# Group 0: when GpSimd's third masking of V starts, and who copies the transposed weights

## The chip, the cores and the metric

One core of a Trainium2 chip runs the whole program. Its engines are TensorE (PE: matmuls and transposes), VectorE (DVE), ScalarE (ACT), GpSimd (POOL) and SyncE (SP, which here only issues DMAs). Each engine works through its own queue in order and waits on semaphores for the others. The metric is the device time of one execution in microseconds (us); the number used is the median over several executions.

## The reference

Attention over keys and values that are pooled eight to one, followed by a two-layer network with a tanh GELU:

```python
k_p = k.reshape(B, H, Sp, pool, D).mean(axis=3)          # B=8, H=8, S=576, D=64, pool=8, Sp=72
v_p = v.reshape(B, H, Sp, pool, D).mean(axis=3)
scores = scale * np.matmul(q, k_p.transpose(0, 1, 3, 2))
attn = np.exp(scores - np.max(scores, axis=-1, keepdims=True))
attn = attn / (np.sum(attn, axis=-1, keepdims=True) + 1e-09)
attn_out = np.matmul(attn, v_p)
x = attn_out.transpose(0, 2, 1, 3).reshape(B * S, H * D)  # 4608 x 512
h = x @ w_in                                              # 512 x 2048
g = 0.5 * h * (1.0 + np.tanh(c * (h + 0.044715 * h * h * h)))
out = g @ w_out                                           # 2048 x 512
```

## The kernel before

The 4608 tokens are cut into nine groups of 512: group g < 8 holds the first 512 tokens of batch g, and a ninth group holds the 64 tokens left over from each batch. A group goes through attention and then through the two layers. Attention of the next group is threaded between the matmuls of the running group by hand: `at(hooks, s, f, ...)` places a call before matmul step s, and the whole program is issued in exactly the order written (`manual_schedule`). For group 0 there is nothing to thread it between, so its attention (lines 689 to 738) is the start-up of the kernel, and TensorE reaches the first layer only when it is through.

In group 0 the 512 queries are worked in four blocks j of 128, two blocks at a time (a half). For each block:

- `cast_q` turns queries into bf16, `q_transpose_pe(g, j, eng, tag)` transposes four 128x128 pieces on TensorE into PSUM (`tp`), and `eng` copies them to `qT`.
- `scores(g, j)` makes four matmuls into `sc`, and `exps(g, j)` lets ScalarE write `e`, the exponentials of eight heads with 72 keys each (128x576).
- `norm_two(g, j, 5)` (lines 284 to 294): VectorE sums `e` (`den`, L264), takes the reciprocal (`r`, L289) and scales the first five heads into `eb` (L291, 128x360); ScalarE scales the other three heads (L294, three instructions).
- `e_transpose_pe(g, j, eng, tag)` (lines 299 to 303) transposes the normalised weights `eb` in five pieces on TensorE, and `eng` copies them to `eT`. A copy is L94 on VectorE or GpSimd and L92 on ScalarE, whatever is copied.
- `values_half(0, 0, x, ...)` multiplies `eT` of blocks 0 and 1 with `vbd` into `xo`; x = 0 uses slots 0 to 3 of `vbd`, x = 1 slots 4 to 7. `xo` is copied to `xT`, from which the first layer (L394, `hidden_half`) starts.

`vbd` is the pooled V, laid out block-diagonally by heads. `spread_v` (lines 167 to 185) makes it with five multiplications by a 0/1 mask (each times 1/8 for the mean): part 0 is two of them, part 1 is one (the third masking), part 2 the last two. For group 0 they run on GpSimd.

The order of GpSimd's queue around the change is: two `w_in` loads, part 0, part 1, the cast of the queries of blocks 2 and 3, part 2, two more `w_in` loads (quarters 2 and 3 of the first layer's weights). The first layer uses quarter 2 in its third stretch of 16 matmuls, and quarter 3 in its fifth. TensorE's queue is: transposes of weights 0, of queries 2 and 3, of weights 1, `scores(0, 2)`, `values_half` for x = 0 and 1, `scores(0, 3)`, first layer. PSUM tiles with tag "mm" rotate through four buffers, so the order of the calls also sets who waits for whose buffer.

SyncE's loads of group 1 wait on line 748, a tiny DMA that reads quarter 1 of `w_in` and writes the tile `gate`. The tile `gate` is elsewhere the target of one-element copies on GpSimd which exist only to make GpSimd wait for what they read (`cast_gated`, `spread_gated`, `gate_queries`).

Of the kernel before, what the change touches and what calls it, by code (L numbers as in the profile page):

```python
# [19 lines left out]
def kernel(  # L20
# [21 lines left out]
    nc = tc.nc  # L42
# [8 lines left out]
    W = H * Sp  # L51
# [18 lines left out]
    eb = consts.tile([128, 4, 5 * 128], BF16, name="eb")  # L70
# [10 lines left out]
    gate = consts.tile([128, 1], BF16, name="gate")  # L81
# [8 lines left out]
    def copy(eng, out, in_):  # L90
        if eng is nc.scalar:
            eng.copy(out=out, in_=in_)  # L92
        else:
            eng.tensor_copy(out=out, in_=in_)  # L94
# [33 lines left out]
    def cast_q(g, j0, j1, eng):  # L128
        if "qb" not in st[g]:
            st[g]["qb"] = work.tile([128, 4, H, D], BF16, name="q_b", bufs=1)  # L130
        copy(eng, st[g]["qb"][:, j0:j1], st[g]["q"][:, :, j0:j1].rearrange("p h j d -> p j h d"))
# [22 lines left out]
    def pool_pe(b, c0, c1, copies, eng):  # L154

        n = c1 - c0
        ps = psum.tile([128, 2, D], F32, name="vp", tag="mm", bufs=4)
        for i in range(8):
            nc.tensor.matmul(out=ps[:, 0:n], lhsT=identf, rhs=st[b]["kv"][:, c0:c1, i, :], start=(i == 0), stop=(i == 7))  # L159
        kvb = st[b]["kvb"]  # L160
        copy(eng, kvb[:, c0:c1, 0:copies, :], ps[:, 0:n].unsqueeze(2).to_broadcast([128, n, copies, D]))
# [5 lines left out]
    def spread_v(b, eng, parts=(0, 1, 2)):  # L167
        kvb = st[b]["kvb"]

        def mult(n0, n1, c0, t0, p0):  # L170
            m = (n1 - n0) // 2
            eng.tensor_tensor(out=vbd[p0:128, b, n0:n1, :].rearrange("p (c r) (hh d) -> p c (r hh) d", c=max(m, 1), d=D),  # L172
                              in0=kvb[p0:128, 4 + c0:4 + c0 + max(m, 1), 0, :].unsqueeze(2).to_broadcast(
                                  [128 - p0, max(m, 1), 4 if m else 2, D]),
                              in1=vmask[p0:128, c0:c0 + max(m, 1), t0:t0 + (4 if m else 2)].unsqueeze(3).to_broadcast(
                                  [128 - p0, max(m, 1), 4 if m else 2, D]), op=ALU.mult)

        if 0 in parts:
            mult(0, 1, 0, 2, 64)
            mult(1, 3, 1, 0, 0)  # L180
        if 1 in parts:
            mult(3, 5, 2, 0, 0)
        if 2 in parts:
            mult(5, 7, 3, 0, 0)
            mult(7, 8, 4, 0, 0)
# [37 lines left out]
    def q_transpose_pe(g, j, eng, tag):  # L223
        tp = psum.tile([128, HP, 128], BF16, name="tp", tag=tag, bufs=BUFS[tag])
        for pr in range(HP):
            nc.tensor.transpose(out=tp[:, pr, :],
                                in_=st[g]["qb"][:, j, 2 * pr:2 * pr + 2, :].rearrange("p h d -> p (h d)"),
                                identity=identb)
        copy(eng, st[g]["qT"][:, j], tp)
# [5 lines left out]
    def scores(g, j):  # L235
        sc = psum.tile([128, 2, MAIN], F32, name="sc", tag="sc", bufs=2)
        qT = st[g]["qT"]
        for pr in range(HP):
            if g == 0:
                o = sc[:, pr // 2, 2 * Sp * (pr % 2):2 * Sp * (pr % 2) + 2 * Sp]  # L240
                nc.tensor.matmul(out=o, lhsT=qT[:, j, pr, :], rhs=kbd[:, g, pr].rearrange("d hh s -> d (hh s)"),
                                 start=True, stop=True)
                continue

            for hh in range(2):
                for p0 in (0, 64):
                    h0 = 64 * hh
                    nc.tensor.matmul(out=sc[p0:p0 + 64, hh, Sp * pr:Sp * pr + Sp],  # L248
                                     lhsT=qT[h0:h0 + 64, j, pr, p0:p0 + 64],
                                     rhs=kbd[h0:h0 + 64, g if g < B else 2 * j + p0 // 64, pr, hh],  # L250
                                     start=True, stop=True)
        st[g][("sc", j)] = sc
# [31 lines left out]
    def norm_two(g, j, h0):  # L284

        e = st[g][("e", j)]
        sums(g, j)
        r = work.tile([128, H], F32, name="r")
        nc.vector.reciprocal(out=r, in_=st[g].pop(("den", j)))  # L289
        o = eb[:, j, 128 * 5 - W:].rearrange("p (h s) -> p h s", s=Sp)  # L290
        nc.vector.tensor_tensor(out=o[:, 0:h0], in0=e[:, 0:h0], in1=r[:, 0:h0].unsqueeze(2).to_broadcast([128, h0, Sp]),  # L291
                                op=ALU.mult)
        for h in range(h0, H):
            nc.scalar.activation(out=o[:, h], in_=e[:, h], func=ACT.Copy, scale=r[:, h:h + 1])  # L294
# [4 lines left out]
    def e_transpose_pe(g, j, eng, tag):  # L299
        tp = psum.tile([128, 5, 128], BF16, name="tp", tag=tag, bufs=BUFS[tag])  # L300
        for c in range(5):
            nc.tensor.transpose(out=tp[:, c, :], in_=eb[:, j, 128 * c:128 * c + 128], identity=identb)
        copy(eng, st[g]["eT"][:, j], tp)
# [412 lines left out]
    norm_two(0, 0, 5)  # L716
    spread_v(0, nc.gpsimd, (0,))
    pool_pe(0, 7, 9, 1, nc.scalar)
    spread_v(0, nc.gpsimd, (1,))
    cast_q(0, 2, 4, nc.gpsimd)  # L720
    spread_v(0, nc.gpsimd, (2,))
    load_w_in(2)
    load_w_in(3)
    norm_two(0, 1, 5)
    e_transpose_pe(0, 0, nc.scalar, "mm")
    q_transpose_pe(0, 2, nc.vector, "mm")
    q_transpose_pe(0, 3, nc.scalar, "mm")
    e_transpose_pe(0, 1, nc.vector, "mm")
    scores(0, 2)
    exps(0, 2)  # L730
    for x in range(2):
# [214 lines left out]
```

## Time and profile before

| What | Value |
|---|---|
| median of 4 runs | 279.49 us (278.79 to 280.01) |
| the profiled execution's own time | 278.79 us |
| its span, first to last instruction | 276.9 us |
| TensorE busy (PE), share of the span | 269.3 us, 97% |
| VectorE busy | 223.6 us, 81% |
| ScalarE busy | 175.9 us, 64% |
| GpSimd busy | 80.3 us, 29% |
| TensorE clock granted, mean | 1.000 |

The profile is of one execution. Its page has the engines' busy time, the span cut into 40 slices, the chain of work that ended last, and the costliest groups of instructions. A group's line reads: program line, engine, operation, tile written <- tile read, shape, count. The trace behind it gives single instructions by time. These lines of the page show how the first of 40 slices (6.9 us each) differ from the rest, in tenths of busy time for each engine:

```profile
PE   7989999999999999999999999999999999999995
DVE  5886869999966799989998999899989558955832
ACT  1586576488546764696479646963696469656820
POOL 4740272006420542314231426663223300300000
PEclk9999999999999999999999999999999999999999
```

TensorE is below nine tenths only in the first slices, 0 to about 21 us, and at the very end. The change lies between 12 and 17 us.

### The profile page before, as it was taken

How to read it: one execution, taken by the hardware profiler on the slowest of the kernel's cores; microseconds unless marked ns; L12 is line 12 of the kernel's file. 1: busy time of each engine (PE TensorE's matmuls, PEld its weight loads, DVE VectorE, ACT ScalarE, POOL GpSimd, SP SyncE). 2: the span in 40 equal slices, each digit the busy share in tenths (PEclk: the TensorE clock that was granted, in tenths of full speed). 3: DMA queues.
4: the chain of work that ended last, by engine and by line, in shares of the span. 5: the costliest groups of instructions: out<-in, count | busy, mean ns of one | idle time of the engine just before them, and what ended most of it. 6: DMA issues, size and time to landing. Idle time of an engine off the chain costs nothing.

```text
span 276.9 us, 6571 instructions
## 1 busy us (share of the span) xinstructions
PE 269.3 (97%) x2686; PEld 192.2 (69%) x2686; DVE 223.6 (81%) x365; ACT 175.9 (64%) x265; POOL 80.3 (29%) x121
## 2 busy tenths in 40 slices
PE   7989999999999999999999999999999999999995
PEld 3668844446854587668866876687668966886684
DVE  5886869999966799989998999899989558955832
ACT  1586576488546764696479646963696469656820
POOL 4740272006420542314231426663223300300000
PEclk9999999999999999999999999999999999999999
DMA  7999999999999896899479969995852460243013
GB/s 228 311 197 284 367 386 228 285 369 227 252 200 244 260 279 140 177 315 228 133 169 286 264 128 216 220 246 153 175 154 47 125 151 2 50 101 100 1 41 114
DMA packets 67857, 54.37 MB, mean 196 GB/s; under 512 B 41459, under 2 KB 53747, under 8 KB 67827
## 3 DMA queue, kind: packets, MB, share of 16 engines
q1 hardware_dynamic: 65186, 50.67, 71.3%
q0 software_dynamic: 2496, 3.15, 6.4%
q8 instruction: 21, 0.34, 0.5%
q10 hardware_dynamic: 144, 0.13, 0.1%
q14 instruction: 10, 0.07, 0.1%
HBM read 36.70 MB, written 9.44 MB: 167 GB/s over the span
## 4 chain that ended last, share of the span: by engine, by line
PE 86%; DVE 7%; DMA 4%; ACT 2%; issue 1%; SPq 0%; DVEq 0%; ACTq 0%
PE mm L586 28%; PE mm L383 22%; PE c L474 13%; PE mm L399 5%; PE mm L394 5%; PE xo L344 3%; PE x L586 3%; PE sc L248 2%; DMA eT<-eb 2%; DMA kv<-in_k_dram 2%; DVE den L264 1%; PE mm L531 1%; PE vp L159 1%; DVE eb L279 1%; ACT gT L490 1%; PE xo L355 1%
## 5 line engine op out<-in xcount | busy, mean ns | idle before, releaser
L383 PE MATMUL mm<-xT,w_in_b 128*128 128x512 bf16 x304 | 69.9, 379 | 0.0
L586 PEld LDWEIGHTS <-gT 128*128 128x128 bf16 x512 | 48.3, 98 | 9.1 <-issue 1.4
L385 ACT ACTIVATE gT<-mm 128x512 bf16<-128x512 f32 x76 | 43.6, 599 | 14.9 <-PE mm L383 14.6
L383 PEld LDWEIGHTS <-w_in_b 128*128 128x128 bf16 x304 | 29.8, 98 | 30.7
L586 PEld LDWEIGHTS <-stage 128*128 128x128 bf16 x384 | 37.5, 98 | 4.6 <-DVE stage L438 0.2
L279 POOL TENSOR_TENSOR eb<-e,r 128x576 bf16<-128x576 f32 x14 | 16.1, 1151 | 58.1 <-DVE r L273 46.1
L92 ACT CAST xT<-xo 128x512 bf16<-128x512 f32 (+1 forms) x24 | 13.2, 610 | 29.0 <-PE xo L344 24.6
L586 PE MATMUL mm<-tw,gT 128*128 128x256 bf16 x240 | 30.0, 273 | 0.0
L586 PE MATMUL mm<-w_out_b,gT 128*128 128x256 bf16 x240 | 29.9, 273 | 0.0
L264 DVE TENSOR_REDUCE den<-e 128x8 f32<-128x576 f32 x36 | 26.2, 727 | 2.9 <-ACT e L257 2.9
L257 ACT ACTIVATE e<-sc 128x576 f32<-128x576 f32 x36 | 22.5, 650 | 8.8 <-POOL eb L279 7.0
L149 DVE TENSOR_TENSOR kv<-kv 128x1024 f32<-128x1024 f32 (+3 forms) x19 | 23.7, 1247 | 4.2 <-DMA kv<-in_k_dram 3.1
L586 PE MATMUL mm<-tw,stage 128*128 128x256 bf16 x224 | 26.7, 273 | 0.0
L92 ACT COPY osb<-mm 128x512 f32<-128x512 f32 x30 | 17.8, 592 | 13.0 <-PE mm L586 12.4
L172 POOL TENSOR_TENSOR vbd<-kvb,vmask 128x256 bf16<-128x256 bf16 (+2 forms) x38 | 22.6, 616 | 7.3 <-DVE kvb L152 6.3
L474 PEld LDWEIGHTS <-ws 128*128 128x128 bf16 x192 | 18.8, 98 | 6.1
L94 POOL CAST q_b<-q_sb 128x1024 bf16<-128x1024 f32 (+1 forms) x15 | 15.6, 1058 | 20.3 <-DMA q_sb<-in_q_dram 20.3
L279 DVE TENSOR_TENSOR eb<-e,r 128x576 bf16<-128x576 f32 x18 | 18.0, 1002 | 0.6
L474 PE MATMUL c<-tt,ws 128*128 128x256 bf16 x144 | 17.7, 273 | 0.0
L434 DVE TENSOR_TENSOR stage<-gT 128x512 bf16<-128x512 bf16 (+1 forms) x25 | 13.2, 528 | 4.1 <-ACT gT L385 2.4
L435 DVE TENSOR_TENSOR gT<-gT 128x512 bf16<-128x512 bf16 (+1 forms) x25 | 13.0, 519 | 3.5 <-ACT gT L385 1.4
L94 POOL COPY kbd<-kTd 64x288 bf16<-64x288 bf16 x12 | 6.1, 504 | 33.2 <-DMA kTd<-kvb 32.9
(107 smaller groups left out, 424.2 us busy)
## 6 DMA issues: line engine op xcount, KB each, us to landing
kv<-in_k_dram SPq DMA_DIRECT2D x7, 1024.0 KB, 8.2
q_sb<-in_q_dram SPq DMA_DIRECT2D x7, 1024.0 KB, 10.1
kv<-in_v_dram SPq DMA_DIRECT2D x6, 1024.0 KB, 9.5
out_dram<-osb SPq DMA_DIRECT2D x12, 512.0 KB, 3.0
out_dram<-osb SPq DMA_DIRECT2D x11, 256.0 KB, 3.3
kv<-in_v_dram SPq DMA_DIRECT2D x4, 512.0 KB, 10.2
w_in_b<-in_moe_w_in_dram POOLq DMA_DIRECT2D x4, 512.0 KB, 6.8
w_out_s<-in_moe_w_out_dram SPq DMA_DIRECT2D x2, 1024.0 KB, 13.2
```

The source lines that it names most:

```text
L92: eng.copy(out=out, in_=in_)
L94: eng.tensor_copy(out=out, in_=in_)
L149: add(out=t[:, :, 0:4, :], in0=t[:, :, 0:4, :], in1=t[:, :, 4:8, :], op=ALU.add)
L172: eng.tensor_tensor(out=vbd[p0:128, b, n0:n1, :].rearrange("p (c r) (hh d) -> p c (r hh) d", c=max(m, 1), d=D), in0=kvb[p0:128, 4 + c0:4 + ...
L257: nc.scalar.activation(out=e.rearrange("p (x h) s -> p x (h s)", x=2), in_=sc[:, :, 0:4 * Sp], func=ACT.Exp, scale=1.0 / 64.0)
L264: nc.vector.reduce_sum(out=den, in_=e, axis=AX.X)
L279: eng.tensor_tensor(out=o.rearrange("p (pr hh s) -> p hh pr s", hh=2, s=Sp), in0=e.rearrange("p (hh pr) s -> p hh pr s", hh=2), in1=r.rear ...
L383: nc.tensor.matmul(out=hp, lhsT=w_in_b[:, ko, fo * 128:(fo + 1) * 128], rhs=st[g]["xT"][:, ko, :], start=(i == 0), stop=(i == KO - 1))
L385: nc.scalar.activation(out=gT[:, fo, :], in_=hp, func=ACT.Gelu_apprx_tanh)
L394: nc.tensor.matmul(out=hp[:, f, :], lhsT=w_in_b[:, ko, (fo + f) * 128:(fo + f + 1) * 128], rhs=st[g]["xT"][:, ko, c0:c0 + 256], start=(ko ...
L474: nc.tensor.matmul(out=acc[:, m, :], lhsT=lhs(i, m), rhs=rhs(i), start=bool(fresh and i == 0 and m % 2 == 0), stop=(i == 1), skip_group_ch ...
L586: nc.tensor.matmul(out=xs[p] if acc is xs else acc[:, p, :], lhsT=lt, rhs=rt, start=bool(fresh and m == 0 and (p == 0 or (last and acc is ...
```

## The change

A one-element copy on GpSimd is put ahead of the third masking. It reads the first element (head 0, key 0) of block 0's normalised weights in `eb`, which VectorE's first normalisation writes. So GpSimd's third masking, and everything behind it in GpSimd's queue, starts after that normalisation. Further, the transposes of the weights of blocks 0 and 1 are called one after the other, ahead of those of queries 2 and 3; the copy of block 0's goes from ScalarE to VectorE, and that of block 1's from VectorE to ScalarE.

```diff
     norm_two(0, 0, 5)
     spread_v(0, nc.gpsimd, (0,))
     pool_pe(0, 7, 9, 1, nc.scalar)
+    nc.gpsimd.tensor_copy(out=gate, in_=eb[:, 0, 128 * 5 - W:128 * 5 - W + 1])
     spread_v(0, nc.gpsimd, (1,))
     cast_q(0, 2, 4, nc.gpsimd)
     spread_v(0, nc.gpsimd, (2,))
     load_w_in(2)
     load_w_in(3)
     norm_two(0, 1, 5)
-    e_transpose_pe(0, 0, nc.scalar, "mm")
+    e_transpose_pe(0, 0, nc.vector, "mm")
+    e_transpose_pe(0, 1, nc.scalar, "mm")
     q_transpose_pe(0, 2, nc.vector, "mm")
     q_transpose_pe(0, 3, nc.scalar, "mm")
-    e_transpose_pe(0, 1, nc.vector, "mm")
     scores(0, 2)
     exps(0, 2)
```

## The prediction, made before the changed kernel ran

> **What bounds the kernel now.** I read the chain of waits first. From 23 us to the end it is nearly all TensorE (86% of the span by the page), with no wait on a load, so whatever moves the first `xo` of group 0 moves the end by the same amount. Start in us, length in us, engine, tile and line:
>
> ```profile
> 12.37 0.98 DVE eb L291
> 13.35 0.67 DVE den L264
> 14.04 0.21 DVE r L289
> 14.30 0.05 issue
> 14.34 0.84 ACT eb L294 x3
> 15.19 0.58 ACT eT L92
> 15.76 0.49 ACT qT L92
> 16.26 0.04 issue
> 16.30 0.62 PE xo L317 x4
> ```
>
> The reader is to see that VectorE's two normalisations (L291) with a sum and a reciprocal between them set the pace, and that `xo` starts at 16.30. It also needs the second block's transposed weights, whose VectorE copy ends at 16.24. Second, the timeline of VectorE and GpSimd over the same stretch, and two later places with the same operations:
>
> ```profile
> 12.37 0.98 DVE L291 TENSOR_TENSOR eb<-e,r 128x360 bf16<-128x360 f32 x1
> 13.27 0.74 DVE L264 TENSOR_REDUCE den<-e 128x8 f32<-128x576 f32 x1
> 14.28 0.92 DVE L291 TENSOR_TENSOR eb<-e,r 128x360 bf16<-128x360 f32 x1
> 18.57 0.76 DVE L276 TENSOR_TENSOR eb<-e,r 128x576 bf16<-128x576 f32 x1
> 38.68 1.36 DVE L279 TENSOR_TENSOR eb<-e,r 128x576 bf16<-128x576 f32 x1
> ```
>
> ```profile
> 12.35 0.61 POOL L172 TENSOR_TENSOR vbd<-kvb,vmask 128x256 bf16<-128x256 bf16 x1
> 13.18 1.07 POOL L94 CAST q_b<-q_sb 128x1024 bf16<-128x1024 f32 x1 [0.21 <-DMA q_sb<-in_q_dram]
> 14.21 0.61 POOL L172 TENSOR_TENSOR vbd<-kvb,vmask 128x256 bf16<-128x256 bf16 x1
> 15.41 1.55 POOL L654 DMA_DIRECT2D w_in_b<-in_moe_w_in_dram  x2
> 38.39 1.04 POOL L94 CAST w_out_b<-w_out_s 128x1024 bf16<-128x1024 f32 x1
> ```
>
> A normalisation of 576 takes 0.76 with GpSimd idle (18.57), but one of only 360 takes 0.98 and 0.92 beside a masking. Scaling by VectorE's f32 additions (128x512 0.69, 128x256 0.42: 1.05 ns an element and 0.15 fixed) 360 elements are worth 0.53. So the two lose 0.45 and 0.39. The loss is a wait, not a slower rate: 12.37 + 0.45 = 12.82, which is 0.14 before the masking's recorded end (12.96); 14.28 + 0.39 = 14.67, 0.15 before 14.82. At 38.68 the partner is a cast: 1.36 - 0.76 = 0.60 of wait ends at 39.28, again 0.15 before its end (39.43). The sum (L264) keeps its 0.74 beside a cast. So I read: whichever of GpSimd's operation and VectorE's two-input operation starts first finishes, the other waits; 0.02 us of lead (12.35 against 12.37) was enough.
>
> **The change part by part.**
>
> *The hold.* The third masking no longer starts at 12.35. The first normalisation then runs clean: 12.37 to 12.90, a gain of 0.45. Sum, reciprocal and second normalisation follow with the old spacing (its start was 0.93 after the first's end): 13.83.
>
> *The new copy into `gate`* is one instruction on GpSimd. Existing one-element copies begin 0.07 after the VectorE result they wait for (75.04 to 75.11), last 0.18 (64x1 bf16) or 0.25 (128x1 f32) undisturbed, 0.59 when VectorE is in a two-input operation, and the next GpSimd operation follows 0.27 after the start of the 0.18 one. In the new order VectorE is in the sum then, so I take 0.27 and keep 0.59. Behind it in GpSimd's queue wait the third masking, the cast of the queries 2 and 3 (whose data land at 13.18, so it loses its old start), two maskings and two `w_in` loads with all that needs them. Third masking 12.97 + 0.27 = 13.24, cast 0.57 later (the step of 11.78 to 12.35): **13.81**, end 14.86.
>
> *The second normalisation meets the cast.* It wants to start at 13.83, the cast at 13.81. That is closer than I can call exactly, so both ends:
> (a) cast first: VectorE waits to 14.86 - 0.15 = 14.71 and ends at 15.24, against 15.20 before. The gain of 0.45 is gone at once.
> (b) VectorE first: it ends at 14.36; ScalarE's three pieces end at 14.73 (reciprocal ends 0.45 earlier, and so do they, bar the 0.01 by which ScalarE comes free). The cast is pushed to 14.36 - 0.13 + 1.05 = 15.28 (0.13 from the masking at 46.65, which sat behind the addition of 46.42).
> A gate of 0.59 gives third masking 13.56, its hold to 14.02, normalisation to 14.55, cast end 15.47: like (b), 0.19 later.
>
> *The new order of transposes and copies.* No instruction is added; weights of block 1 now stand before the queries in TensorE's queue. With T the end of the second normalisation: weights' transposes at T + 0.06 (15.20 to 15.26 before), issue 0.27 for five, then query 2's; first transpose to the start of its copy 0.43 (9.09 to 9.52), VectorE's copy 0.41, +0.06 to `scores(0, 2)` (15.54 to 15.60), four matmuls 0.24, then `xo`. So `xo` = T + 0.06 + 0.27 + 0.43 + 0.41 + 0.06 + 0.24 = T + 1.47, where it was T + 1.10. Before, the query copy (15.13 to 15.54) lay in the shadow of the second normalisation; now it is behind it: **0.37 given away** whatever T is. ScalarE's copy of block 1 (0.67) starts at T + 0.06 + 0.49 and ends at T + 1.22, hidden behind the query path; VectorE's copy of block 0 (0.49) ends near T + 0.45, hidden too. Were the query path shorter, `xo` could not start before T + 1.28.
> (a): 15.24 + 1.47 = 16.71, **+0.41**. (b): queries' transposes wait for the cast, 15.28 + 0.05 (14.25 to 14.30 before) + 0.43 + 0.41 + 0.06 + 0.24 = 16.47, +0.17; with the long gate +0.36.
> I take (a), because the gate's nearest row puts the cast ahead and a lead of 0.02 decided before.
>
> *The last two maskings* start behind the normalisation in (a) and end near 16.2; the `xo` that needs them comes at 17.1, so they cost nothing with 0.9 of cover.
>
> *The two `w_in` loads* go from 15.41 to about 16.15 (0.75 later). Nothing moved passes SP's queue: its wait is for the second `w_in` quarter, issued at 10.37 ahead of all this. Time from issue to landing of third and fourth quarter:
>
> ```profile
> w_in_b<-in_moe_w_in_dram POOLq DMA_DIRECT2D x1, 512.0 KB, 6.0
> w_in_b<-in_moe_w_in_dram POOLq DMA_DIRECT2D x1, 512.0 KB, 9.9
> ```
>
> The fourth (issued 16.16) lands at 26.06. Its first matmul comes 32 matmuls of 0.109 after 23.03: 26.52, and 26.93 with the +0.41. Shifted by 0.75 it lands at 26.8: nothing lost, cover 0.1. The third lands at 21.4 for use at 23.03: cover 1.6. Below nothing: an earlier landing gains nothing, as TensorE doesn't wait for it today.
>
> Sum in the profiled execution: span 276.9 + 0.41 = 277.3; its own time is 278.79 (1.9 outside the span), so 279.2. That execution was the fastest of the four; the median is 279.49, so 279.49 + 0.41 = **279.9**.
>
> One rule speaks against this change. The Trainium skill, SBUF — State Buffer, section "Who interferes with whom": VectorE with two SBUF inputs and a reading GpSimd contend for one port pair, the first to issue keeps it for the whole instruction. The rows above show such waits, but ending 0.15 before the recorded end; by the rule's letter the wait in (a) would last to 14.86 and the sum would be +0.56, an estimate.
>
> **Rivals.**
> 1. *VectorE first* (b): 279.49 + 0.17 = 279.7, up to 279.85 with the long gate. For it: 0.02 us between two starts. Against: the gate would have to take longer than its nearest row.
> 2. *Not slower: the casts share instead of blocking.* If the cast did not hold up the second normalisation and was not held up itself, T would be ScalarE's 14.73 and `xo` 16.20: -0.10, 279.4; were the query copy also off the path, T + 1.28 gives 16.01 and 279.2. It decides from T + 1.47 < 16.30, that is T below 14.83. Against it stands the 1.36 at 38.68.
> 3. *The fourth `w_in` quarter comes late.* While only the `w_in` queue ran (20.3 to 20.5: 100% of the traffic) it moved about 205 packets a us; next to the loads of group 1, from 22.3 on, about half of that. If the 0.75 lost is made up at half speed, landing is 26.06 + 1.50 = 27.56, 0.63 after 26.93: +1.04 in all, 280.5. For it: a cover of 0.1. Against: at 17.6 that queue had run dry for about 0.3 us, so part of the delay is only idling moved, and most packets of the last quarter were through by 23.8; a single straggler made the 26.06. It decides from a landing after 26.93.
> The Trainium skill, DMA: Bandwidth & Descriptors, section "Queues, rings and completion order", has each DMA engine take turns between queues; if the loads issued at 18.72 shared from about 20, as that would have it, the landing would be near 28.2 and the total near 281.2, an estimate. The trace has them start only after 21.9.
> 4. *The hold does not free the first normalisation* (ScalarE's reads of the same `e` slow it, not GpSimd): T = 15.20 or later, with the cast 0.45 later still, xo 16.7 to 17.1, 279.9 to 280.3. Against: at 40.97 a normalisation ran in 0.76 beside a ScalarE cast.
>
> **How the numbers follow.** Chances: forecast 0.42, rival 1 0.18, rival 2 0.13, rival 3 0.17, rival 4 0.10. 0.3% is 0.84 us, about what a measurement of this kernel can tell from no change; the four times before spread over 1.2 us, so I give each case +-0.4. Slower by over 0.84: nearly all of rival 3, a tenth of the forecast and a little of rival 4: 0.24. Faster by over 0.84: the tail of rival 2: 0.05. Same: 0.71. Range: from rival 2 with its spread, 279.1, to rival 3's 280.8.
>
> **What would show it.** In the new profile: first L291 near 0.53, second near 1.4 (forecast), near 0.53 with a cast over 1.4 (rival 1), 0.9 with a normal cast (rival 2); query 2's copy after block 0's copy on VectorE; `xo` of group 0 at 16.7; the fourth `w_in` load landing before 26.9 with no gap on TensorE at L394. Wrong would be a gate copy of another length, or a TensorE wait on a load.

## The result, and the profile after

The changed kernel takes 280.17 us at the median (39 runs), the kernel before 279.42 us (60 runs). The ratio is 1.0027, with a 95% interval from 1.0017 to 1.0038: **0.75 us slower, between 0.5 and 1.1**. The forecast was +0.41. The two executions of the changed kernel above 283 us, and one of 286.39 us of the kernel with late loads below, fell in a slower state and are left out of the ratios.

| | before | after |
|---|---|---|
| median | 279.42 us | 280.17 us |
| profiled execution, own time | 278.79 us | 282.13 us |
| its span | 276.9 us | 280.2 us |

The profiled execution of the changed kernel is one of its slowest; its spans go from 276.9 to 281.2 us, so the profile shows an extreme of what happens, not the typical size. It also starts 0.24 us later: the first sum of `e` begins at 11.59 instead of 11.35. Both have to be kept apart from the change.

First the timeline of VectorE and GpSimd after, for the lines that were shown of before (start, length, engine, line, operation):

```profile
12.61 0.53 DVE L291 TENSOR_TENSOR eb<-e,r 128x360 bf16<-128x360 f32 x1
13.06 0.74 DVE L264 TENSOR_REDUCE den<-e 128x8 f32<-128x576 f32 x1
...
14.07 1.25 DVE L291 TENSOR_TENSOR eb<-e,r 128x360 bf16<-128x360 f32 x1
15.25 0.48 DVE L94 COPY eT<-tp 128x640 bf16<-128x640 bf16 x1
16.10 0.42 DVE L94 COPY qT<-tp 128x512 bf16<-128x512 bf16 x1 [0.37 <-PE tp L226]
```

```profile
13.21 0.19 POOL L719 COPY gate<-eb 128x1 bf16<-128x1 bf16 x1 [0.58 <-DVE eb L291]
13.35 0.61 POOL L172 TENSOR_TENSOR vbd<-kvb,vmask 128x256 bf16<-128x256 bf16 x1
13.90 1.04 POOL L94 CAST q_b<-q_sb 128x1024 bf16<-128x1024 f32 x1
14.90 1.26 POOL L172 TENSOR_TENSOR vbd<-kvb,vmask 128x256 bf16<-128x256 bf16 x2
16.10 1.56 POOL L654 DMA_DIRECT2D w_in_b<-in_moe_w_in_dram  x2
```

The first normalisation runs clean (0.53), as the hold is meant to do. The second meets the cast: 14.07 + 1.25 = 15.32, and 1.25 - 0.53 = 0.72 of it is waiting, until 14.79, which is 0.15 before the cast's end (13.90 + 1.04 = 14.94). Query 2's copy now lies behind the normalisation, not in its shadow. `xo` starts at 16.84; without the 0.24 of the later start that is 16.60 against 16.30 before.

Then the chain of waits after, in the same stretch:

```profile
12.61 0.54 DVE eb L291
13.15 0.05 issue
13.21 0.19 POOL gate L719
13.40 0.56 POOL vbd L172
13.96 0.98 POOL q_b L94
14.94 1.22 POOL vbd L172 x2
16.16 0.75 POOL w_in_b L654
16.91 12.51 DMA w_in_b<-in_moe_w_in_dram
29.42 0.05 issue
29.46 1.59 PE mm L394 x13
```

This is what the reader is to see: the chain no longer goes through the second normalisation and `xo` at all. It goes through the new gate copy, down GpSimd's queue, to the issue of the fourth `w_in` quarter, and from there to its landing at 29.42. Before, that load landed at 26.06, ahead of its use. TensorE's waits in the list of waits between 15 and 40 us (weight loads of the first layer; total, times, longest):

```profile
PEld L394 <- DMA w_in_b<-in_moe_w_in_dram: 2.6, 2, 2.1
```

Why 12.5 us for a load that took 9.9? The DMA traffic between 17.8 and 18.2 us tells it (queue q0 is that of GpSimd's loads, which carries `w_in`; packets, MB, share of the engines' time). Before:

```profile
q0 software_dynamic: 57, 0.06, 95.4%
```

After:

```profile
q0 software_dynamic: 2, 0.00, 8.8%
```

The second quarter is through by then and the third has been issued too late to follow on, so almost nothing moves. Between 17.4 and 19.0 the queue carries 131 packets instead of 269. At the 205 packets a us that it moves alone the difference is worth 0.7 us, of which 0.24 is the later start. It is made up from 22 us on, beside the loads of group 1; from 23.4 to 23.8 each of the two queues then moves 24 to 30 packets. The rest of the 12.5 us is a trickle. From 25.8 to 29.0 GpSimd's queue carries only 2 or 3 packets in each 0.4 us, as it did from 23.8 to 25.8 in the kernel before. So most of the load is about 2 us late and its last packets are 3.4 us late. Why the last packets trickle is not shown.

### The profile page after: what moved, and what is told of

It reads as the page before. It is cut to its first block, busy times and chain, and to the rows that moved or that the text cites. A ratio compares the mean times of both kernels' runs of the same rounds, so it can differ in the third digit from the quotient of the medians.

```text
span 280.2 us, 6572 instructions
## 1 busy us (share of the span) xinstructions
PE 269.3 (96%) x2686; PEld 192.3 (69%) x2686; DVE 221.2 (79%) x365; ACT 176.5 (63%) x265; POOL 80.0 (29%) x122
## 4 chain that ended last, share of the span: by engine, by line
PE 78%; DMA 10%; DVE 7%; POOL 2%; SPq 1%; ACT 1%; issue 0%; DVEq 0%
PE mm L586 29%; PE mm L383 20%; PE c L474 12%; PE mm L399 5%; DMA w_in_b<-in_moe_w_in_dram 4%; PE xo L344 3%; DMA kTd<-kvb 3%; PE mm L394 3%; PE x L586 2%; DMA q_sb<-in_q_dram 2%; PE sc L248 2%; PE mm L531 1%; DVE den L264 1%; DMA eT<-eb 1%; DVE eb L279 1%; ACT gT L490 1%
## 5 line engine op out<-in xcount | busy, mean ns | idle before, releaser
L92 ACT CAST xT<-xo 128x512 bf16<-128x512 f32 (+1 forms) x24 | 13.2, 610 | 27.8 <-PE xo L344 23.8
L149 DVE TENSOR_TENSOR kv<-kv 128x1024 f32<-128x1024 f32 (+3 forms) x19 | 22.7, 1195 | 5.3 <-DMA kv<-in_k_dram 4.1
L92 ACT COPY osb<-mm 128x512 f32<-128x512 f32 x30 | 17.8, 592 | 14.1 <-PE mm L586 13.4
L172 POOL TENSOR_TENSOR vbd<-kvb,vmask 128x256 bf16<-128x256 bf16 (+2 forms) x38 | 22.0, 601 | 8.5 <-DVE kvb L152 7.5
L394 PE MATMUL mm<-xT,w_in_b 128*128 128x256 bf16 x128 | 15.7, 273 | 2.2 <-DMA w_in_b<-in_moe_w_in_dram 2.1
L279 DVE TENSOR_TENSOR eb<-e,r 128x576 bf16<-128x576 f32 x18 | 17.1, 949 | 0.6
```

What stands on the lines that cost most here:

```text
L149: add(out=t[:, :, 0:4, :], in0=t[:, :, 0:4, :], in1=t[:, :, 4:8, :], op=ALU.add)
L279: eng.tensor_tensor(out=o.rearrange("p (pr hh s) -> p hh pr s", hh=2, s=Sp), in0=e.rearrange("p (hh pr) s -> p hh pr s", hh=2), in1=r.rear ...
L394: nc.tensor.matmul(out=hp[:, f, :], lhsT=w_in_b[:, ko, (fo + f) * 128:(fo + f + 1) * 128], rhs=st[g]["xT"][:, ko, c0:c0 + 256], start=(ko ...
```

## The experiments

Each is compared with runs of the kernel before on the same chip, in five rounds. The intervals are 95% intervals of the ratio. First the two parts of the change by themselves, then the loads alone, then a queue order that keeps them early.

**The hold alone.** Old order of transposes and copies, gate copy kept:

```diff
+    nc.gpsimd.tensor_copy(out=gate, in_=eb[:, 0, 128 * 5 - W:128 * 5 - W + 1])
     spread_v(0, nc.gpsimd, (1,))
```

> The kernel before with the gate copy alone, transposes and copies in their old order. Theory P (port and path): first L291 0.53, cast ahead of the second L291, which waits and ends about 0.1 earlier than in the kernel before; xo of group 0 at T + 1.10, so about 16.2 against 16.30: -0.1. Theory L (late w_in loads): GpSimd issues the third and fourth quarter 0.6 to 0.7 us later, their queue runs dry near 18 us, the fourth quarter lands after its first matmul in many executions, so TensorE waits at L394 and the median is 0.3 to 0.5 us above before all the same. P alone: -0.1 and no wait on w_in. Rival (the order of the copies is the whole loss): no loss here.

Measured: ratio 1.0040 (1.0019 to 1.0061), +1.1 us (0.5 to 1.7). `xo` at 16.38, with a start 0.14 later: -0.06. So the attention of group 0 is no slower, the kernel is, and by no less than with the whole change, as far as the intervals tell. In its profiled execution TensorE does not wait for `w_in`; the loss comes later there (the table below).

**The order alone.** The changed kernel without its gate line, in two sets of runs.

> The changed kernel without the gate copy. P: both L291 as before (0.98 and 0.92), xo at T + 1.47 to 1.52 instead of T + 1.10, so 16.7: +0.35 to +0.4 on the median. L: the w_in loads are issued at 15.4 as before and land in time, no TensorE wait beyond what the kernel before has. Rival (the order costs nothing because TensorE waits for w_in later anyway): 0.0.

> order_alone once more (first time +0.14, with an interval from -0.45 to +0.7), for a narrower interval of the path's price: P says +0.35 to +0.45 from the xo at 16.74, less the 0 to 0.1 us by which starts differ.

Measured: 1.0005 (0.9984 to 1.0026) and 0.9986 (0.9957 to 1.0015). `xo` starts at 16.74 and 16.80, which is the 0.4 that theory P priced, but no loss can be seen at the end: in us the two intervals are -0.4 to +0.7 and -1.2 to +0.4, so the second ends just below the 0.44 to 0.50 by which `xo` moved, and the first holds them. The rival's 0.0 fits, but not its reason: TensorE does not wait for `w_in` in either profile.

**The two loads later, nothing else.**

```diff
+    nc.gpsimd.memset(tw[:, 0, 0:2], 0.0)
+    nc.gpsimd.memset(tw[:, 0, 2:3], 0.0)
     load_w_in(2)
     load_w_in(3)
```

> The kernel before with some 0.75 us of memsets on GpSimd (into tw, which is written only much later) just ahead of the third and fourth w_in load; nothing else moves. L: xo stays at 16.3, the queue of w_in runs dry near 18 us, the fourth quarter lands 0.7 to 3 us later than 26.1 and TensorE waits for it at L394 in many executions: +0.3 to +0.6 on the median and a wider spread. P: no difference, within 0.1.

Measured: 1.0077 (1.0049 to 1.0106), +2.1 us (1.4 to 3.0) from six executions, far above what was expected. The loads are issued at 16.09 instead of 15.41, `xo` is where it was, and between 17.8 and 18.2 the queue carries 7 packets instead of 57. TensorE's timeline from the third stretch of the first layer on, before:

```profile
23.03 9.01 PE L394 MATMUL mm<-xT,w_in_b 128*128 128x256 bf16 x81
```

With late loads:

```profile
23.00 3.66 PE L394 MATMUL mm<-xT,w_in_b 128*128 128x256 bf16 x32
27.32 5.52 PE L394 MATMUL mm<-xT,w_in_b 128*128 128x256 bf16 x49 [0.67 <-ACT gT L396]
33.99 0.20 PE L207 MATMUL kT<-identb,kvb 64*128 64x64 bf16 x1 [0.93 <-DVE kvb L165]
```

There are two waits. The view puts the 0.67 down to ScalarE, whose GELU (26.69 to 27.29) happens to end there. In the same place the weight loads wait 0.9 us for `w_in`, which lands 10.4 us after an issue at about 16.9, so at 27.3. In the kernel before, TensorE runs past this point without a wait, beside the same GELU.

The 0.93 is a wait for the keys of group 1, which SyncE loads. VectorE's first operation on them (L149) starts at 29.17 instead of 28.24. So its last copy (L165) now starts beside a cast of GpSimd. Before:

```profile
31.94 0.18 DVE L165 COPY kvb<-kvb 128x64 bf16<-128x64 bf16 x1
```

With late loads, VectorE and GpSimd:

```profile
32.87 1.06 DVE L165 COPY kvb<-kvb 128x64 bf16<-128x64 bf16 x1
32.86 1.04 POOL L94 CAST q_b<-q_sb 128x1024 bf16<-128x1024 f32 x1 [15.21 <-PE mm L394]
```

**0.68 us of lateness in two DMA issues, with no work on TensorE moved, is enough to cost what the whole change costs, or more.** The hold alone issues them 0.45 later (0.59 less its later start of 0.14) and loses 1.1 us; the two intervals overlap.

**The fourth quarter needed later.** Two stretches of group 0's first layer change places, so that quarter 3 is used 1.75 us later:

```diff
-        for half, c in [(0, 0), (0, 1), (0, 2), (1, 0), (0, 3), (1, 1), (1, 2), (1, 3)]:
+        for half, c in [(0, 0), (0, 1), (0, 2), (1, 0), (1, 1), (0, 3), (1, 2), (1, 3)]:
```

Put into the changed kernel, run beside the changed kernel itself, into the kernel with late loads, and into the kernel before as a control:

> The changed kernel once more, beside the following ones. Theory L (the w_in loads, issued 0.7 us later, leave their queue dry near 18 us and land late): +0.5 to +1.0 on the median, another profile with a TensorE wait at L394 of other length than the 1.8 and 0.25 us of the first, or none. Theory P (path alone): +0.3, no wait.

> The changed kernel with the sixth stretch of the first layer of group 0 (half 1, quarter 1) before the fifth (half 0, quarter 3): the fourth w_in quarter is needed 1.75 us later, all else the same. L: most of the waits go, what is left is the path, xo 0.3 later than in the kernel before: 0.2 to 0.4 above before, and 0.4 or more below after_again. P: the same as after_again. Rival (the loss arises later, in the loads of group 1): the same as after_again.

> loads_late (the kernel before with 0.75 us of memsets ahead of the last two w_in loads, 2.1 us slower) with the same exchange of two stretches. L: of the 2.1 us at least 1.2 come back, so 0 to 0.9 above before. If the 2.1 come from another place (group 1's loads pushed back), it stays near 2.1.

> The kernel before with the exchange of the fifth and sixth stretch alone. L: if some executions of the kernel before wait for the fourth quarter too (26.1 against 26.5 in the profile), the exchange gains 0 to 0.3; it is also the control for the other kernels with the exchange. Rival: the exchange costs something by itself: slower.

| kernel | ratio to before | interval |
|---|---|---|
| changed, again | 1.0050 | 1.0021 to 1.0079 |
| changed, exchange | 1.0022 | 1.0001 to 1.0043 |
| late loads | 1.0077 | 1.0049 to 1.0106 |
| late loads, exchange | 1.0031 | 1.0013 to 1.0049 |
| before, exchange | 0.9978 | 0.9949 to 1.0007 |

With late loads the exchange takes back 1.3 us of 2.1, and the intervals just touch; the two were run in different sets, on different chips, each against the kernel before on its own. With the change, the two intervals overlap; the direction is as expected, the size isn't settled. The control shows no cost of the exchange and perhaps a gain. At its middle value, 0.6 us, that gain would be about half of the 1.3, so the exchange alone doesn't show what the wait at the fifth stretch costs. What the exchange leaves, 0.9 us with late loads, was not expected by a theory that knew only that wait. In the profile of late loads with the exchange TensorE waits for the third quarter instead, which the exchange doesn't move:

```profile
24.05 9.15 PE L394 MATMUL mm<-xT,w_in_b 128*128 128x256 bf16 x81 [0.86 <-DMA w_in_b<-in_moe_w_in_dram]
```

**Where the rest goes.** The start of some matmuls on TensorE, from the timelines of the profiled executions, in us:

```
kernel          xo group 0   second layer   xo group 1   group 1's first   group 2's first   span
                             of group 0                  layer             layer
before             16.30        35.69         48.80         51.60             80.53          276.9
order alone        16.74        36.13         49.24         51.77             80.56          276.7
order again        16.80        36.18         49.29         51.93             80.85          277.0
hold alone         16.38        36.29         49.38         52.02             81.77          278.3
changed            16.84        38.64         51.76         54.28             83.10          280.2
changed again      16.88        36.71         49.82         52.41             81.71          277.9
late loads         16.27        37.49         50.60         53.13             82.44          279.9
load in gap        15.78        35.17         48.29         51.14             79.93          276.4
```

Two things are to be read here. With the order alone the 0.44 of `xo` is still there at `xo` of group 1 and gone by group 2: later waits take it up (the 32 matmuls of that `xo` span 1.46 us before and 1.19 here). In its second profile 0.32 of the 0.50 is left at group 2. The profile of the kernel before with the exchange, whose first layer starts 0.15 later, stands at 81.02 there, 0.49 above the kernel before, so single profiles don't tell such shifts apart. With the hold alone 0.08 at the first `xo` becomes 0.60 at the second layer and 1.24 at group 2. The hold's chain between 50 and 84 us begins

```profile
49.51 8.79 DMA q_sb<-in_q_dram
...
58.70 0.62 ACT q_b L92
```

where the chain of the kernel before is TensorE throughout. That load of group 2's queries is issued at 49.51 in place of 48.76. Followed further back, the chain runs through group 1's attention to SyncE's load of `w_out`, issued at 21.23 and landing at 35.57. In the second run of the changed kernel TensorE's wait at L394 is absent too. The second layer starts 1.02 later; 0.58 of that is `xo` (0.28 a later start), and the rest arises at a wait for group 1's queries. Later the chain passes through the transposed queries of group 2:

```profile
54.31 7.92 PE mm L383 x37
62.23 5.00 DMA qT<-q_b
67.23 0.04 issue
```

TensorE's waits for a load, or for work that waits for one, between 22 and 37 us show where the late `w_in` loads are felt. Beside them stands the start of GpSimd's first cast of `w_out`, which waits for SyncE's load of it (us):

| kernel | TensorE waits | first cast of `w_out` |
|---|---|---|
| before | none | 34.72 |
| order alone | none | 34.70 |
| changed | 0.25 third quarter, 1.82 fourth quarter | 36.34 |
| changed, again | 0.28 group 1's queries | 35.52 |
| changed, exchange | 0.48 `w_out` | 36.08 |
| hold alone | 0.21 group 1's keys, 0.18 `w_out` | 35.62 |
| late loads | 0.67 fourth quarter, 0.93 group 1's keys | 35.54 |
| late loads, exchange | 0.86 third quarter, 0.29 group 1's keys | 36.23 |

In all eight profiles with the `w_in` loads on time that cast starts between 33.85 and 35.08, and TensorE has no such wait. So the late loads cost in two ways, at L394 or through SyncE's loads, which share the DMA engines with them, and sometimes in both.

**The third quarter early, the hold kept.** One part of the change undone:

```diff
     pool_pe(0, 7, 9, 1, nc.scalar)
+    load_w_in(2)
     nc.gpsimd.tensor_copy(out=gate, in_=eb[:, 0, 128 * 5 - W:128 * 5 - W + 1])
...
-    load_w_in(2)
     load_w_in(3)
```

> The changed kernel with one part undone: the third w_in quarter is issued ahead of the gate copy, in GpSimd's wait for the first normalisation; all else stays. Theory L (late loads make most of the loss): the queue of w_in doesn't run dry near 18 us, no TensorE wait on w_in, so only the path's loss is left: -0.1 to +0.3 on the median against before. The load ends near 13.2, so the cast comes 0.05 to 0.2 later than in the changed kernel and now behind VectorE's second L291: that takes 0.53 and the cast 1.4 or more; xo near 16.45. Theory P (the loss is the path): xo in the changed kernel 16.6, here 16.45: +0.15 to +0.3. If the loss comes from neither, it stays at +0.75.

Measured: 1.0037 (1.0006 to 1.0069), +1.0 us (0.2 to 1.9). The expectation failed, though the queue no longer runs dry (82 packets in those 0.4 us) and TensorE does not wait for `w_in`. A new wait took the place. VectorE and GpSimd in this kernel:

```profile
13.80 2.36 DVE L291 TENSOR_TENSOR eb<-e,r 128x360 bf16<-128x360 f32 x1
```

```profile
13.80 1.04 POOL L94 CAST q_b<-q_sb 128x1024 bf16<-128x1024 f32 x1
14.80 0.96 POOL L172 TENSOR_TENSOR vbd<-kvb,vmask 128x256 bf16<-128x256 bf16 x2
```

Both start at 13.80; GpSimd has it, and keeps it for the two maskings behind the cast. The normalisation ends at 16.16; behind the cast alone it would have ended near 15.22 (14.84 - 0.15 + 0.53). TensorE has nothing to do from 13.8 to 16.2, and after that its granted clock falls: it is 0.50 from 18 to 21 us. The stretches of this kernel (us; busy time and count of PE, PEld, DVE, ACT, POOL; PEclk; DMA share, GB/s):

```profile
12.00:17.00 5.00, 2.55 (x32) 2.30 (x30) 4.50 (x8) 2.25 (x8) 4.53 (x8) 1.00 1.25 208
17.00:24.00 7.00, 6.70 (x56) 5.47 (x54) 4.69 (x9) 5.52 (x9) 0.00 (x0) 0.76 1.19 249
```

The eight matmuls of `xo` take 1.86 us there instead of 1.05. The mean clock over the span is 0.994 in 7 of its 12 executions. The same 0.993 to 0.994 stands in 4 of the 39 executions of the changed kernel, and 0.992 in 2 of 35 of the kernel before on the same chip as this run; that these are the same wait was not shown.

**The third quarter in GpSimd's idle gap, no hold.** The kernel before with one new order of GpSimd's queue:

```diff
     pool_pe(0, 7, 9, 1, nc.scalar)
-    spread_v(0, nc.gpsimd, (1,))
-    cast_q(0, 2, 4, nc.gpsimd)
-    spread_v(0, nc.gpsimd, (2,))
-    load_w_in(2)
+    load_w_in(2)
+    cast_q(0, 2, 4, nc.gpsimd)
+    spread_v(0, nc.gpsimd, (1,))
+    spread_v(0, nc.gpsimd, (2,))
     load_w_in(3)
```

> A new order of GpSimd's queue in the kernel before: third w_in quarter in the gap before the queries land (12.4 to 13.2), then the cast, then third to fifth masking, then the fourth quarter. No gate, old order of transposes. P: no masking beside the first L291, so 0.53; the second meets the end of the cast and waits some 0.25, T is set by ScalarE at about 14.75; xo at T + 1.10 = 15.85: -0.45. L: the third quarter is issued 3 us earlier and the fourth no later than before, so the queue doesn't run dry: no TensorE wait on w_in, median 0.4 to 0.5 us below before. If issuing a load holds the port as a masking does, the first L291 stays near 0.9 and only 0 to -0.1 is left.

> load_in_gap once more, to confirm the version below both kernels: 0.4 to 0.7 us below before.

> load_in_gap (0.6 us below before) with the exchange. L: the fourth quarter lands at 25.5 there, just ahead of its first matmul at 26.0, so a few executions may wait; the exchange takes these away: 0 to 0.3 below load_in_gap, so 0.6 to 0.9 below before. Rival: the exchange does nothing: 0.6.

Measured: 0.9978 (0.9960 to 0.9997) and again 0.9960 (0.9930 to 0.9989), 0.6 and 1.1 us below before; with the exchange 0.9977 (0.9950 to 1.0004), so nothing more. This version beats both kernels. Its VectorE lines:

```profile
12.42 0.53 DVE L291 TENSOR_TENSOR eb<-e,r 128x360 bf16<-128x360 f32 x1
...
13.89 0.75 DVE L291 TENSOR_TENSOR eb<-e,r 128x360 bf16<-128x360 f32 x1
14.73 0.42 DVE L94 COPY qT<-tp 128x512 bf16<-128x512 bf16 x1
15.23 0.49 DVE L94 COPY eT<-tp 128x640 bf16<-128x640 bf16 x1
```

The first normalisation is clean without any gate, since GpSimd only issues a load beside it; the second waits 0.22 for the end of the cast. `xo` is at 15.78, 0.52 earlier, and the load queue stays full (81 packets between 17.8 and 18.2). How much of the gain is the shorter stall and how much the full queue was not run apart.

## Why the prediction was right or wrong

- **The hold frees the first normalisation**: right, 0.53.
- **The gate copy at 0.27 to the next operation**: off. It lasts 0.19, and the masking follows 0.14 after its start.
- **The second normalisation loses to the cast (a)**: right, and the size with it: it waits until 0.15 before the cast's end. T came at 15.08 (15.32 less the later start of 0.24), 0.16 before the 15.24 worked out; 0.13 of that is the cheaper gate.
- **The new order gives 0.37 away**: right for `xo`: T + 1.52 against T + 1.47 worked out. Sum for `xo` +0.30 instead of +0.41, mostly by the gate.
- **"whatever moves the first `xo` of group 0 moves the end by the same amount"**: this step failed. The hold alone moves `xo` by -0.06 and the end by +1.1; the late loads move `xo` by nothing and the end by +2.1. The chain of one execution had no load on it, but loads stood close behind. Whether a later `xo` is paid in full at the end stays open: the order alone moves `xo` by 0.44 to 0.50 and the end by nothing that can be seen, but one of its intervals reaches +0.7, and with the load in the gap 0.52 off `xo` goes with 0.6 and 1.1 off the end.
- **"nothing lost, cover 0.1" for the fourth `w_in` quarter**: the other step that failed, and the one that carries the loss. Issued 0.75 later than before (0.51 without the late start), it landed 3.4 later in the profiled execution, and in the other profiles with late loads 0.1 to 3.3 later. The shift was taken as a shift; but the queue ran dry, and the missing packets went through later, beside group 1's loads. The cover of 1.6 for the third quarter was not safe either: it landed at 23.9 instead of 21.4 and TensorE waited 0.25 for it. Rival 3 had this mechanism, with +1.04 in all and a chance of 0.17; it took the dry queue before (17.6) for slack, when it was a sign that the queue had no reserve. It also looked for the loss at L394 alone; the hold alone loses 1.1 us with no wait there in its profile.
- **"Nothing moved passes SP's queue"**: true of the issues (the first at 18.93 against 18.72, no more than the later start), but not of the landings. SyncE's loads share the DMA engines with the late quarters, and the first cast of `w_out` starts 0.8 to 1.6 later in the six profiles with late loads. The sum had no term for this.
- So +0.75 is near the forecast's +0.41 partly by chance: the price that was put on the order of the copies can't be found at the end, and a price that was put at zero is paid.
- **The range, 279.1 to 280.8**: with the spread of 0.4 that is stated, rival 2's 279.4 and rival 3's 280.5 give 279.0 to 280.9. Nothing hangs on it.
- **Rival 2 (sharing)** is out by the 1.25; **rival 1 (VectorE first)** did not happen in any of the profiles of these kernels, though with the third quarter early both started at 13.80.

What stays open: how the loss divides between the wait at L394 and SyncE's loads. That the late issue alone is enough for it is shown by the late loads and the hold alone; both ways can be read in single profiles, but the exchange, with its control, is too uncertain to price either, and for the change itself the intervals are too wide to divide 0.75.

## What to carry to other kernels

When work is pushed back in a queue that also issues loads, count the issues behind it first, and look at whether the load queue has anything left at the moment the next issue is due: here 0.7 us of delay in two issues cost 2.1 us (1.4 to 3.0) in one kernel, and 0.45 us cost 1.1 (0.5 to 1.7) in another. A stall that is moved by a hold comes back at the next pair of operations that use the same port; filling the gap with something that leaves the port alone, such as issuing a load early, removed it at the first normalisation here and left 0.22 at the second. And a chain of waits without loads in one execution doesn't say that loads have slack: check how far behind their landings are.

## What the runs showed of the hardware

- VectorE's two-input f32 operation waits for a GpSimd operation that has begun, until 0.13 to 0.15 us before its recorded end, in the seven cases worked out from these profiles. It can wait for more than the one in flight: for a cast and two maskings, 2.36 us instead of 0.53, when both started at 13.80. In the changed kernel, where the cast led by 0.17, it came in right behind the cast. The Trainium skill, SBUF — State Buffer, section "Who interferes with whom", says that the first to issue keeps the shared ports for the whole instruction; here VectorE had issued before the two maskings and still came after them, so the measurement decides.
- A VectorE copy with one input can be held in the same way: 128x64 bf16 took 1.06 us beside a GpSimd cast that had started 0.01 earlier, and 0.18 in the kernel before.
- After about 2.4 us with TensorE idle (13.8 to 16.2) the granted clock averaged 0.76 from 17 to 24 us, and 0.50 from 18 to 21.
- In the kernel before, SyncE's first loads of group 1, issued from 18.7 on, moved almost nothing before 22 us, while GpSimd's queue had packets; at the start of the program, with no other traffic, packets moved about 1 us after the issue. What held them back is not shown.
